# Filter spectra padded from 84 to 98 partitions with zeros

## The chip, the cores and the metric

One core of a Trainium2 chip runs the kernel. The metric is the device time in microseconds (us) of one execution. The engines are PE (TensorE), DVE (VectorE), ACT (ScalarE), POOL (GpSimd) and the queue of SP, which here only issues DMAs.

## What is computed

The reference, cut to what matters (B = 2, S = 12480, D = 128):

```python
h_filt = (np.maximum(pos_emb @ w1, 0.0) @ w2) * np.exp(-0.01 * pos)[:, None]
u = x * v
Uf = np.fft.rfft(u, n=2 * S, axis=1)
Hf = np.fft.rfft(h_filt, n=2 * S, axis=0)
y = np.fft.irfft(Uf * Hf[None], n=2 * S, axis=1)[:, :S, :]
a = (x * y).reshape(B * S, D)
h = a @ moe_w_in
out = (np.maximum(h, 0) + moe_alpha * np.minimum(h, 0)) @ moe_w_out
```

A long convolution of two sequences u with a filter h_filt, channel by channel, a gate, and then a two-layer network over 24,960 tokens.

## The kernel before, in words

The convolution is done with Fourier transforms written as matrix products. Time is split as t = 128 p + i; p lies on partitions, i along the free axis. A sequence u needs NT = 98 values of p. The filter falls by exp(-1.28) from one p to the next and is kept for HT = 84 values of p, so its operands have 84 partitions where those of u have 98. Each number is held as a high and a low half of 16 bits, so that each product is three matmuls.

The 128 channels are done in two groups (g = 0, 1) of 64. For each group there are three stages:

- **Stage 1** (`stage1`) takes "chunks" of four channels. `u_pair` loads x and v, multiplies them (L678), sums squares (ACT L681, PE L689), finds a scale (DVE L695, L332 to L334), scales (L706), and splits into halves (ACT L712, L715). `h_chunk` does a chunk of the filter. Both end in `transform`: twelve matmuls over partitions (L750 to L752; the data are the stationary operand, the table `t1` the moving one, 180 columns), then ACT writes the high half of the result to the tile `z` (L762) and DVE the low half (L765).
- **Stage 2** (`stage2`, L836 to L841) transforms over i with tables `tw` that are loaded as it goes, and multiplies by the spectrum of the filter (DVE L864, L874, POOL L869); L887 and L891 write the product back to `z`.
- **Stage 3** (`stage3`, PE L965 to L967, ACT L977, L979, DVE L982) goes back over i and stores to `g_d` in DRAM.

A group has 32 chunks of u and 16 of the filter. For g = 0 the filter is computed first (`filter_`, PE L463 to L465); its 64 channels of group 0 are left in a part of `z` that stage 1 fills later (`hz`), and those of group 1 are stored to DRAM (`h_d`, L512, four stores from a tile `hst` that is used twice). In g = 0 the 16 filter chunks come in one run between the two halves of u. In g = 1, stage 1 runs beside stage 3 of g = 0, and its filter chunks are loaded from `h_d` (L736) and come singly between those of u. From about 600 us to the end runs the two-layer network (phase B, L1219 and L1298 to L1306).

The order of the work of stages 1 and 3 on each engine is written by a planner, `Plan`: each operation is given to it with its engine, an assumed duration, what it reads and what it writes; it simulates the engines and emits the operations in the order of their simulated starts. Each engine runs its own list in order. `Plan.op` has an argument `rows` (128 unless given): for a PE operation the simulated clock is 2.4 or 1.2 GHz by the work that the simulated PE did shortly before, weighted by `rows / 128`. `pace` in `phase_a` gives each kind of work its place.

Of the kernel before, what the change touches and what calls it, by code (L numbers as in the profile page):

```python
# [24 lines left out]
NI = 128  # L25
# [262 lines left out]
def body(ctx, tc, A, out, stop=None, dbg=None):  # L288
# [27 lines left out]
    early = {}  # L316
    ring = const.tile([128, 25 - FIRST, 512], F32, name="ring")

    h_d = dram.tile([CG // CC, HT, 2, CC * NI], F16, name="h_d")
    w_d = dram.tile([NFT // 4, 128, 4, 4, 128], F16, name="w_d")  # L320
    wo_d = dram.tile([NFT // 4 - 1, 128, 512], F32, name="wo_d")
    g_d = dram.tile([64 // IDX, NF, B * D // W3, IDX * 4 * W3], F32, name="g_d")
# [17 lines left out]
    def filter_(P, pool, z, zw, mm, mb):  # L340
# [12 lines left out]
        nq_ = pool.tile([128, 16], F32, bufs=1, name="nq")  # L353
        n1 = pool.tile([128, 1], F32, bufs=1, name="n1")
        nb = pool.tile([128, 128], F32, bufs=1, name="nb")
        ac.dma_start(out=w1b, in_=A["w1b"])
        ac.dma_start(out=w2b, in_=A["w2b"])
        po.tensor_tensor(out=w2q, in0=w2b[:, 0], in1=w2b[:, 1], op=ALU.add)
# [146 lines left out]
        for x in range(2):  # L505
            for q in range(4):
                final(CG + x * HC, HC, q, dst, [("hs", 0, q), ("hs", 1, q)])
                yield
            n0 = x * HC // CC
            for h in range(2):  # L510
                def store(n0=n0, h=h):
                    sy.dma_start(out=h_d[n0:n0 + HC // CC, :, h, :].rearrange("n p e -> p n e"),  # L512
                                 in_=hst[h].rearrange("p (n c) i -> p n (c i)", c=CC))
                P.op("DMA", dma_ns(HT * HC * NI * 2), store, r=[("hs", h, q) for q in range(4)], w=[("h_d", x, h)])

# [120 lines left out]
    def phase_a():  # L636
# [15 lines left out]
        def stage1(P, g, shared, U):  # L652
            def u_pair(n):

                nps = P.buf("m")
                more = not shared and n >= NCH // 2 and n // 2 % 2
                kind = ("x2", "v2", "sq1", "uhl2") if more else ("x", "v", "sq1", "uhl")
                x, v, sq = [P.buf(kind[0]) for _ in range(2)], [P.buf(kind[1]) for _ in range(2)], P.buf(kind[2])
                b, c = divmod(n * CC, CG)
                c += g * CG  # L660
                s = s_u[:, b, c:c + 2 * CC]

                def xr(j):
                    return units(U[x[j].pool][x[j].i], p=NT)

                def vr(j):
                    return units(U[v[j].pool][v[j].i], p=NT)

                def sqr():
                    return units(U[sq.pool][sq.i], p=NT).bitcast(BF16).rearrange("p (c i) -> p c i", i=NI)  # L670

                for j in range(2):
                    def load(j=j):
                        sy.dma_start(out=xr(j), in_=A["xv"][g, n + j, :, 0, :])
                        sy.dma_start(out=vr(j), in_=A["xv"][g, n + j, :, 1, :])

                    def product(e, j=j):
                        either[e].tensor_tensor(out=xr(j), in0=xr(j), in1=vr(j), op=ALU.mult)  # L678

                    def square(j=j):  # L680
                        ac.activation(sqr()[:, j * CC:j * CC + CC].rearrange("p c i -> p (c i)"), xr(j), AF.Square)  # L681

                    P.op("DMA", dma_ns(2 * NT * 2048), load, r=stored if more else [], w=[x[j], v[j]])
                    P.op({"DVE": dve_ns(512), "POOL": 1225}, 0, product, r=[v[j]], w=[x[j]])
                    P.op("ACT", act_ns(512), square, r=[x[j], sq], w=[("sq", n, j)])

                def norm():
                    for m in range(8):
                        te.matmul(mb[nps.i][:, :128], ones[:NT], sqr()[:, :, 16 * m:16 * m + 16], start=m == 0, stop=m == 7)  # L689

                def spare(j):
                    return mb[nps.i][:, 256 + 2 * CC * j:256 + 2 * CC * (j + 1)]

                def gather():
                    ve.tensor_reduce(out=spare(0), in_=mb[nps.i][:, :128].rearrange("p (c e) -> p c e", e=16), op=ALU.add, axis=AX.X)  # L695

                def scale():
                    scales(spare(1), spare(0), s)

                P.op("PE", 450, norm, r=[sq, ("sq", n, 0), ("sq", n, 1)], w=[nps], rows=98)  # L700
                P.op("DVE", 220, gather, r=[nps], w=[("s", g, n)])
                P.op("DVE", 450, scale, r=[nps], w=[("s", g, n)])
                for j in range(2):
                    def scaled(e, j=j):
                        u = xr(j).rearrange("p (c i) -> p c i", c=CC)
                        either[e].tensor_tensor(out=u, in0=u, op=ALU.mult,  # L706
                                                in1=s[:NT, j * CC:(j + 1) * CC].unsqueeze(2).to_broadcast([NT, CC, NI]))

                    h = P.buf(kind[3])

                    def high(j=j, h=h):
                        ac.activation(halves(h)[:, 0], xr(j), AF.Copy)  # L712

                    def low(e, j=j, h=h):
                        either[e].tensor_tensor(out=halves(h)[:, 1], in0=xr(j), in1=halves(h)[:, 0], op=ALU.subtract)  # L715

                    P.op({"DVE": 600, "POOL": 1001}, 0, scaled, r=[("s", g, n)], w=[x[j]])
                    P.op("ACT", act_ns(512), high, r=[x[j]], w=[h])
                    P.op({"DVE": 600, "POOL": 1113}, 0, low, r=[x[j]], w=[h])
                    transform(n + j, [h], split(h))  # L720
# [7 lines left out]
            def h_chunk(n):  # L728
                if not shared:
                    c0 = n * CC  # L730
                    hz = z[:HT, NU // ZC:].rearrange("p b h a f c -> p b (h a f) c")
                    transform(n, [("hz", h, q) for h in range(2) for q in range(8)],
                              lambda c, part: hz[:, (c0 - NU) // ZC, part * NI:(part + 1) * NI, c0 % ZC + c])
                    return
                h = P.buf("uhl")
                P.op("DMA", dma_ns(HT * 2048), lambda: sy.dma_start(out=halves(h, HT), in_=h_d[n - NCH]), w=[h])  # L736
                transform(n, [h], split(h, HT))

            def transform(n, keys, data):
                pb = P.buf("mm")  # L740
                col = n * CC
                zb, cs = z[:, col // ZC], slice(col % ZC, col % ZC + CC)
                late = [("rs", x) for x in range(8)] if not shared and CG <= col < NU else []

                def product():
                    p = mm[pb.i].rearrange("p (c j) -> p c j", c=CC)
                    rows = HT if n >= NCH else NT
                    for c in range(CC):
                        o = p[:, c, :2 * NF]
                        te.matmul(o, data(c, 0), t1[:rows, 0], start=True, stop=False)  # L750
                        te.matmul(o, data(c, 0), t1[:rows, 1], start=False, stop=False)  # L751
                        te.matmul(o, data(c, 1), t1[:rows, 0], start=False, stop=True)  # L752

                def pv():
                    return mm[pb.i].rearrange("p (c j) -> p c j", c=CC)[:, :, :2 * NF].rearrange("p c (a f) -> p a f c", a=2)

                P.op("PE", 12 * 84, product, r=keys, w=[pb] + late, rows=98)

                cuts = (0, 2 * FB, NF) if n == NCH - 1 or shared and n == NC // CC - 1 else (0, NF)
                for x, y in zip(cuts, cuts[1:]):  # L760
                    def high(x=x, y=y):
                        ac.activation(zb[:, 0, :, x:y, cs], pv()[:, :, x:y], AF.Copy)  # L762

                    def low(x=x, y=y):
                        ve.tensor_tensor(out=zb[:, 1, :, x:y, cs], in0=pv()[:, :, x:y], in1=zb[:, 0, :, x:y, cs], op=ALU.subtract)  # L765

                    P.op("ACT", act_ns(8 * (y - x), True), high, r=[pb], w=[("z", n, x)])
                    P.op("DVE", dve_ns(8 * (y - x)), low, r=[pb], w=[("z", n, x)])
# [175 lines left out]
        def stage3(P, g, places, sines_at, y, tap=None):  # L944
            for q in range(NU // W3):
# [6 lines left out]
                for h in range(W3 // 4):  # L952
# [32 lines left out]

                    for i0, i1 in ((1, 2), (2, 64)) if tap and q == NU // W3 - 1 else ((1, 64),):
                        P.op("ACT", 2 * act_ns(4 * (i1 - i0), True) + 70 * (i0 == 1), lambda i=(i0, i1), f=sines: f(*i),
                             r=[pb, gb, *(y[1] if q == ZC // W3 - 1 else ())], w=[(sb_, i0), ("g", r, 2, i0)])
                        for k, op in enumerate((ALU.add, ALU.subtract)):
                            P.op("DVE", dve_ns(8 * (i1 - i0)), lambda k=k, op=op, i=(i0, i1), f=both: f(k, op, *i),  # L990
                                 r=[pb, sb_, (sb_, i0), gb], w=[("g", r, k, i0)])
# [415 lines left out]
```

## Time and profile before

| | us |
|---|---|
| median of three runs | 1719.01 |
| lowest and highest | 1716.59 to 1724.47 |
| profiled execution, its own time | 1721.53 |
| its span, first to last instruction | 1719.7 |

The span holds stage 1 of g = 0 from the start to about 162 us, stage 2 to about 285, stages 1 and 3 together to about 420, stage 2 of g = 1 to about 535, the last stage 3 to about 600, and phase B. In rows of the trace "84*128 84x180" is a matmul whose stationary operand has 84 partitions and 128 columns and whose moving one has 84 partitions and 180 columns. PEclk is the granted clock of TensorE as a share of 2.4 GHz: 1.00 and 0.50 are its two levels, and what lies between is a mean over a stretch that has both.

### The profile page before, as it was taken

The page shows a single profiled execution, that of the slowest core. Times are in us where ns is not written, and L with a number is a line of the kernel's source. Part 1 is how long each engine was busy: PE and PEld are TensorE (multiplying, and loading weights), DVE is VectorE, ACT ScalarE, POOL GpSimd, SP SyncE. Part 2 cuts the span into 40 slices and gives each one's busy share as a digit, 9 for nine tenths or more (in the row PEclk, how much of TensorE's full clock was granted, in tenths as well). Part 3 has the DMA queues.
Part 4 walks back from the last instruction along what each step waited for, and adds up shares of the span by engine and source line. Part 5 has one row for each costly group of instructions (what it writes and reads, how often), then busy time and mean ns, then how long its engine had stood idle before and what let it go on. Part 6 is the DMA issues. An engine that isn't in the chain of part 4 may idle for free.

```text
span 1719.7 us, 34460 instructions
## 1 busy us (share of the span) xinstructions
PE 1597.5 (93%) x13452; PEld 1128.3 (66%) x13452; DVE 1406.8 (82%) x1946; ACT 1342.8 (78%) x2227; POOL 972.6 (57%) x689
## 2 busy tenths in 40 slices
PE   6888888889888899999999999999999999999998
PEld 3887878888778756655565556555655565556654
DVE  5867998976988778888888888888888887888786
ACT  5766776776785488888888888888888888888886
POOL 5565887885895055445544554555444554555443
PEclk9867999997999999999999999999999999999999
DMA  7342334775443941120220212202202022022100
GB/s 202 109 127 93 130 123 148 219 216 165 154 150 99 245 110 52 40 54 20 72 54 20 54 37 56 54 20 61 63 22 54 20 72 54 20 54 57 36 10 20
DMA packets 95571, 144.63 MB, mean 84 GB/s; under 512 B 7187, under 2 KB 63861, under 8 KB 93967
## 3 DMA queue, kind: packets, MB, share of 16 engines
q1 hardware_dynamic: 94287, 141.72, 28.3%
q8 instruction: 105, 1.72, 0.4%
q10 hardware_dynamic: 1120, 0.70, 0.1%
q14 instruction: 59, 0.48, 0.1%
HBM read 100.39 MB, written 42.01 MB: 83 GB/s over the span
## 4 chain that ended last, share of the span: by engine, by line
PE 60%; DVE 16%; ACT 8%; issue 7%; DMA 6%; POOL 2%; SPq 0%; POOLq 0%; ACTq 0%; DVEq 0%
PE hp L1219 25%; PE o L1219 22%; DVE ring L864 4%; DVE ring L1299 4%; ACT ring L1298 3%; DVE ring L874 3%; DMA first<-in_xv 2%; ACT g_hi L1305 2%; PE mm L752 1%; DMA g_d<-ring 1%; PE mm L750 1%; PE mm L751 1%; PE yp L278 1%; PE yp L280 1%; PE yp L279 1%
## 5 line engine op out<-in xcount | busy, mean ns | idle before, releaser
L1219 PEld LDWEIGHTS <-w 128*128 128x128 f16 x6144 | 590.2, 97 | 444.2 <-issue 35.3
L1306 POOL TENSOR_TENSOR g_lo<-ring,g_hi 128x780 f16<-128x780 f32 x256 | 442.6, 1729 | 546.7 <-ACT g_hi L1305 546.5
L1299 DVE SCALAR_TENSOR_TENSOR ring<-ring,keep,hp 128x780 f32<-128x780 f32 x512 | 524.1, 1024 | 188.8 <-ACT ring L1298 182.2
L1298 ACT ACTIVATE ring<-hp 128x780 f32<-128x780 f32 x512 | 419.1, 819 | 169.1 <-PE hp L1219 168.3
L1219 PE MATMUL hp<-ah,w 128*128 128x390 f16 x2048 | 506.2, 328 | 15.2 <-DVE ring L1299 14.1
L1219 PE MATMUL o<-g_hi,w 128*128 128x390 f16 x2048 | 504.4, 328 | 0.7 <-ACT ot L1320 0.7
L1305 ACT ACTIVATE g_hi<-ring 128x780 f16<-128x780 f32 x512 | 434.0, 848 | 2.7 <-DVE ring L1299 0.8
L1306 DVE TENSOR_TENSOR g_lo<-ring,g_hi 128x780 f16<-128x780 f32 x256 | 330.2, 1290 | 0.0
L1219 PE MATMUL hp<-alo,w 128*128 128x390 f16 x1024 | 253.3, 328 | 0.8 <-DVE alo L1211 0.8
L1219 PE MATMUL o<-g_lo,w 128*128 128x390 f16 x1024 | 252.6, 328 | 0.6 <-POOL g_lo L1306 0.6
L1181 POOL TENSOR_TENSOR gl<-gt,gh 90x1024 f16<-90x1024 f32 x62 | 132.7, 2141 | 0.0
L864 DVE TENSOR_TENSOR ring<-mm,ring 128x512 f32<-128x512 f32 (+2 forms) x188 | 115.9, 656 | 15.4 <-ACT ring L852 14.7
L891 POOL TENSOR_TENSOR z<-ring,z 128x512 f16<-128x512 f32 x88 | 110.5, 1256 | 7.2 <-ACT z L887 7.2
L765 DVE TENSOR_TENSOR z<-mm,z 128x720 f16<-128x720 f32 (+1 forms) x99 | 85.7, 878 | 33.1 <-ACT z L762 32.8
L965 PE MATMUL mm<-t,z 128*128 128x128 f16 x512 | 103.5, 234 | 8.2 <-DVE ring L982 3.9
L750 PE MATMUL mm<-t,ring 98*128 98x180 f16 (+1 forms) x320 | 88.3, 278 | 24.5 <-DVE z L765 7.7
L869 POOL TENSOR_TENSOR ring<-ring 128x256 f32<-128x256 f32 (+1 forms) x90 | 80.6, 896 | 48.4 <-DVE ring L864 40.1
L762 ACT ACTIVATE z<-mm 128x720 f16<-128x720 f32 (+1 forms) x99 | 74.2, 756 | 39.4 <-PE mm L752 39.1
L966 PE MATMUL mm<-t,z 128*128 128x128 f16 x512 | 102.9, 233 | 0.0
L967 PE MATMUL mm<-t,z 128*128 128x128 f16 x512 | 102.8, 233 | 0.0
L982 DVE TENSOR_TENSOR ring<-mm,ring 90x504 f32<-90x504 f32 (+2 forms) x132 | 80.7, 656 | 22.7 <-ACT ring L979 21.9
L715 POOL TENSOR_TENSOR ring<-ring 98x512 f16<-98x512 f32 x63 | 79.1, 1272 | 27.8 <-ACT ring L712 24.6
(186 smaller groups left out, 2999.2 us busy)
## 6 DMA issues: line engine op xcount, KB each, us to landing
g_d<-ring SPq DMA_DIRECT2D x32, 720.0 KB
gt<-g_d SPq DMA_DIRECT2D x16, 1440.0 KB
ring<-in_tw SPq DMA_DIRECT2D x34, 512.0 KB
ring<-in_xv SPq DMA_DIRECT2D x72, 196.0 KB
xt<-in_xt SPq DMA_DIRECT2D x31, 390.0 KB
out_t<-ot SPq DMA_DIRECT2D x31, 390.0 KB
first<-in_xv SPq DMA_DIRECT2D x56, 196.0 KB
first<-in_tw SPq DMA_DIRECT2D x12, 512.0 KB
```

The source lines that it names most:

```text
L750: te.matmul(o, data(c, 0), t1[:rows, 0], start=True, stop=False)
L864: ve.tensor_tensor(out=t[:, :, m], in0=p[:, :, m], in1=hs[:, a:a + 1, m].to_broadcast([128, 2, (b1 - b0) * 2 * ZC]), op=ALU.mult)
L891: e.tensor_tensor(out=zl, in0=v, in1=zh, op=ALU.subtract)
L965: te.matmul(o, hi, t3[:, 0], start=True, stop=False)
L966: te.matmul(o, hi, t3[:, 1], start=False, stop=False)
L967: te.matmul(o, lo, t3[:, 0], start=False, stop=True)
L1181: po.tensor_tensor(out=dl, in0=src, in1=dh, op=ALU.subtract)
L1219: te.matmul(o[:, b, :TOK], w, d[:, b], start=start and n == 0, stop=stop and n == 2)
L1298: ac.activation(neg, h, AF.Relu, scale=-1.0)
L1299: ve.scalar_tensor_tensor(out=acts[n], in0=neg, scalar=keep[:, f:f + 1], in1=h, op0=ALU.mult, op1=ALU.add)
L1305: ac.activation(gh, a, AF.Copy)
L1306: (ve, po)[n % 2].tensor_tensor(out=gl, in0=a, in1=gh, op=ALU.subtract)
```

## The change

The filter's operands are laid out with 98 partitions, the last 14 zero, and all transforms read 98. `hz` is cleared once from partition 64 up at the start (one memset on DVE, one on POOL), before `filter_` writes its 84. `h_d` has 98 partitions, and one more DMA writes zeros to 14 of them. The planner's arguments change too: `rows=98` is dropped for the two PE operations of stage 1, the transform is put down with 78 in place of 84 ns for a matmul, and in `stage3` the wait of ACT for the end of stage 2 (`y[1]`) stands at the second block of eight channels in place of the fourth.

```diff
-    h_d = dram.tile([CG // CC, HT, 2, CC * NI], F16, name="h_d")
+    h_d = dram.tile([CG // CC, NT, 2, CC * NI], F16, name="h_d")
...
+        zero = pool.tile([NT - HT, 2 * CC * NI], F16, bufs=1, name="zero")
+        po.memset(zero, 0.0)
+        for b, e in ((0, ve), (1, po)):
+            e.memset(zw.bitcast(F32)[64:, (NU // ZC + b) * 2 * NF * ZC:][:, :NI * ZC], 0.0)
...
+            if x == 0:
+                P.op("DMA", dma_ns((NT - HT) * CG * NI * 4), lambda: sy.dma_start(
+                    out=h_d[:, HT:].rearrange("n p h e -> p n (h e)"),
+                    in_=zero.unsqueeze(1).to_broadcast([NT - HT, CG // CC, 2 * CC * NI])), r=[("hs", 0, 0)], w=[("h_d", 2, 0)])
...
-                    sy.dma_start(out=h_d[n0:n0 + HC // CC, :, h, :].rearrange("n p e -> p n e"),
+                    sy.dma_start(out=h_d[n0:n0 + HC // CC, :HT, h, :].rearrange("n p e -> p n e"),
...
-                P.op("PE", 450, norm, r=[sq, ("sq", n, 0), ("sq", n, 1)], w=[nps], rows=98)
+                P.op("PE", 450, norm, r=[sq, ("sq", n, 0), ("sq", n, 1)], w=[nps])
...
-                    hz = z[:HT, NU // ZC:].rearrange("p b h a f c -> p b (h a f) c")
+                    hz = z[:NT, NU // ZC:].rearrange("p b h a f c -> p b (h a f) c")
...
-                P.op("DMA", dma_ns(HT * 2048), lambda: sy.dma_start(out=halves(h, HT), in_=h_d[n - NCH]), w=[h])
-                transform(n, [h], split(h, HT))
+                P.op("DMA", dma_ns(NT * 2048), lambda: sy.dma_start(out=halves(h), in_=h_d[n - NCH]), w=[h])
+                transform(n, [h], split(h))
...
-                        te.matmul(o, data(c, 0), t1[:rows, 0], start=True, stop=False)
+                        te.matmul(o, data(c, 0), t1[:, 0], start=True, stop=False)
...
-                P.op("PE", 12 * 84, product, r=keys, w=[pb] + late, rows=98)
+                P.op("PE", 12 * 78, product, r=keys, w=[pb] + late)
...
-                             r=[pb, gb, *(y[1] if q == ZC // W3 - 1 else ())], w=[(sb_, i0), ("g", r, 2, i0)])
+                             r=[pb, gb, *(y[1] if q == 1 else ())], w=[(sb_, i0), ("g", r, 2, i0)])
```

## Rows read from the trace of the kernel before

**Rows 1.** The page: busy time by engine; granted clock in 40 slices of 43 us.

```profile
PE 1597.5 (93%) x13452; PEld 1128.3 (66%) x13452; DVE 1406.8 (82%) x1946; ACT 1342.8 (78%) x2227; POOL 972.6 (57%) x689
...
PEclk9867999997999999999999999999999999999999
```

**Rows 2.** Stretches: from:to, length, busy us (x instructions) of engines, clock, DMA.

```profile
110.00:120.00 10.00, 10.00 (x72) 10.00 (x70) 4.83 (x6) 5.93 (x9) 3.05 (x3) 0.50 0.11 34
...
140.00:150.00 10.00, 7.69 (x67) 6.87 (x65) 9.90 (x15) 7.60 (x13) 10.00 (x9) 0.75 0.69 237
...
410.00:420.00 10.00, 9.61 (x63) 9.17 (x62) 4.85 (x7) 5.62 (x10) 2.57 (x3) 0.50 0.48 165
...
106.80:133.20 26.40, 26.40 (x187) 26.39 (x186) 14.77 (x28) 15.60 (x24) 14.73 (x14) 0.50 0.10 32
...
309.50:400.40 90.90, 79.73 (x1082) 76.43 (x1080) 77.27 (x141) 66.64 (x156) 75.52 (x64) 0.97 0.77 224
```

**Rows 3.** Groups by shape, 104 to 133.2 us: busy us, mean ns, idle before.

```profile
L752 PE MATMUL mm<-t,z 84*128 84x180 f16 x52 | 18.5, 356 | 0.0
...
L765 DVE TENSOR_TENSOR z<-mm,z 128x720 f16<-128x720 f32 x16 | 14.4, 904 | 10.8 <-ACT z L762 10.7
L762 ACT ACTIVATE z<-mm 128x720 f16<-128x720 f32 x15 | 11.7, 778 | 12.3 <-PE mm L752 12.3
```

**Rows 4.** Timeline of PE: start us, us; a run of 72 matmuls.

```profile
107.86 0.36 PE L750 MATMUL mm<-t,z 84*128 84x180 f16 x1
...
118.50 0.36 PE L752 MATMUL mm<-t,z 84*128 84x180 f16 x1
```

**Rows 5.** Timeline of PE after the filter chunks: two stretches of 98-partition matmuls.

```profile
130.22 0.36 PE L750 MATMUL mm<-t,ring 98*128 98x180 f16 x1
...
134.85 0.24 PE L751 MATMUL mm<-t,ring 98*128 98x180 f16 x1
...
136.63 0.24 PE L750 MATMUL mm<-t,ring 98*128 98x180 f16 x1
...
137.49 0.24 PE L752 MATMUL mm<-t,ring 98*128 98x180 f16 x1
```

**Rows 6.** Timeline of PE, then of DVE, at the gap ahead of the filter chunks.

```profile
101.65 0.31 PE L750 MATMUL mm<-t,ring 98*128 98x180 f16 x1 [4.70 <-DVE z L765]
...
100.08 0.69 DVE L678 TENSOR_TENSOR ring<-ring 98x512 f32<-98x512 f32 x1 [4.41 <-DMA ring<-in_xv]
```

**Rows 7.** Groups by shape, 404 to 419.6 us: busy us, mean ns, idle before.

```profile
L752 PE MATMUL mm<-t,ring 98*128 98x180 f16 x21 | 7.5, 357 | 0.0
...
L765 DVE TENSOR_TENSOR z<-mm,z 128x720 f16<-128x720 f32 x7 | 6.3, 906 | 5.5 <-ACT z L762 5.5
...
L750 PE MATMUL mm<-t,ring 84*128 84x180 f16 x12 | 4.3, 358 | 0.0
```

**Rows 8.** Timeline of PE, SP's queue and DVE at the end of stage 1.

```profile
400.44 0.25 PE L750 MATMUL mm<-t,ring 84*128 84x180 f16 x1 [2.69 <-DMA ring<-h_d]
...
401.92 12.31 SPq L736 DMA_DIRECT2D ring<-h_d  x3
...
422.44 0.43 DVE L532 TENSOR_SCALAR ring<-ring 128x512 int32<-128x512 int32 x1 [1.27 <-DMA ring<-in_wo]
```

**Rows 9.** Timelines of DVE and POOL at the start of the span.

```profile
1.02 0.20 DVE L386 MEMSET z<- 128x176 uint32 x1
5.10 0.51 DVE L405 SCALAR_TENSOR_TENSOR z<-mm,ring 128x336 f32<-128x336 f32 x1 [3.87 <-PE mm L402]
...
12.20 1.26 POOL L678 TENSOR_TENSOR ring<-ring,first 98x512 f32<-98x512 f32 x1 [6.90 <-DMA first<-in_xv]
```

**Rows 10.** The chain in order of time, 60 to 180 us; DMA issues there.

```profile
75.82 5.50 DMA h_d<-ring
...
h_d<-ring SPq DMA_DIRECT2D x4, 672.0 KB
```

**Rows 11.** Timelines of DVE and ACT where stage 3 of g = 0 begins.

```profile
291.52 0.78 DVE L891 TENSOR_TENSOR z<-ring,z 128x384 f16<-128x384 f32 x1
...
292.06 0.66 ACT L977 ACTIVATE ring<-mm 90x252 f32<-90x252 f32 x2 [0.33 <-PE mm L967]
```

More of the change, by code (lines that the diff above doesn't have):

```diff
@@ L746, in product @@
                     p = mm[pb.i].rearrange("p (c j) -> p c j", c=CC)
-                    rows = HT if n >= NCH else NT
                     for c in range(CC):
                         o = p[:, c, :2 * NF]
-                        te.matmul(o, data(c, 0), t1[:rows, 0], start=True, stop=False)
-                        te.matmul(o, data(c, 0), t1[:rows, 1], start=False, stop=False)
-                        te.matmul(o, data(c, 1), t1[:rows, 0], start=False, stop=True)
+                        te.matmul(o, data(c, 0), t1[:, 0], start=True, stop=False)
+                        te.matmul(o, data(c, 0), t1[:, 1], start=False, stop=False)
+                        te.matmul(o, data(c, 1), t1[:, 0], start=False, stop=True)
                 def pv():
                     return mm[pb.i].rearrange("p (c j) -> p c j", c=CC)[:, :, :2 * NF].rearrange("p c (a f) -> p a f c", a=2)
-                P.op("PE", 12 * 84, product, r=keys, w=[pb] + late, rows=98)
+                P.op("PE", 12 * 78, product, r=keys, w=[pb] + late)
                 cuts = (0, 2 * FB, NF) if n == NCH - 1 or shared and n == NC // CC - 1 else (0, NF)
```

## The prediction

> **What bounds the kernel now.** I read the page first. PE is busy 93% of the span, but its clock is not high throughout: in the 40 slices it stands at 9 nearly everywhere and falls to 6 and 7 in the third, fourth and tenth [rows 1]. Those slices lie in stage 1 of g = 0 and at the end of stage 1 of g = 1, where the filter's transforms are. So next the busy times by stretch, to see what binds there: from 106.8 to 133.2 us PE is busy for all 26.40 us at 0.50, which is 1.2 GHz, while DVE, ACT and POOL each work for only some 15 us; 410 to 420 looks alike [rows 2]. Then the groups of that first stretch, to see who waits for whom: before the DVE evictions L765 lie 10.8 us of idle time, ended by ACT L762, and before those 12.3 us, ended by PE L752 [rows 3]. That is a loop with PE at its head: PE is the bound, at half its clock. From 140 to 150 us, in the second half of u, it is the other way round, DVE 9.90 and POOL 10.00 of 10 us [rows 2]; a faster PE buys nothing there.
>
> The timeline shows what the clock did. It fell behind a PE gap of 4.70 us, which a late load of x and v opened [rows 6]. Then filter chunks with 84 partitions ran back to back: 72 matmuls from 107.86 to 118.50, one each 10.64/71 = 0.150 us, and the clock did not rise [rows 2, 4]. At 130.22 chunks with 98 partitions took over, equally dense, and 4.6 us later, at 134.85, a matmul lasted 0.24 in place of 0.36 us: the clock had risen [rows 5]. From then twelve matmuls come one each 0.86/11 = 0.078 us [rows 5]. Of what PE did before, the number of partitions is the one plain difference between the two streams.
>
> **The change part by part.**
>
> **The 98 partitions in g = 0.** The count and columns of the matmuls stay. A chunk takes 12 x 0.150 = 1.80 us at the low clock and 12 x 0.078 = 0.94 at the high one [rows 4, 5]. I assume that the gap before 101.65 stays, so the clock still falls, but that the stream which follows now has 98 partitions throughout and lifts it after 4.6 us, at 106.3, in place of 134.85. Of those 28.5 us PE alone would give back 28.5 x (1 - 0.078/0.150) = 13.7. It will not all come: DVE has 14.77 us of work in 26.4, thus about 16 in 28.5, so it becomes the bound and at most 12.5 come back [rows 2]. The upper end is 12.5. The lower: the chunks of u behind the filter must be loaded, scaled and split meanwhile on the same engines, and if they are ready no earlier than now, the gain ends in a wait ahead of them; only what shortens the loads' waits is left, which I bound by a quarter, 3. These products wait in their queues behind the evictions that wait for PE, so most of the chain moves along, and I take 9.0, nearer to the DVE row than to nothing.
>
> **The 98 partitions in g = 1.** From 309.5 to 400.4 the clock is 0.97 [rows 2], so there is next to nothing to get. At 400.44 a gap of 2.69 us, for a filter chunk from DRAM, ends that [rows 8], and up to 419.6 chunks of 98 and 84 partitions alternate at 0.36 us a matmul [rows 7]. With 98 throughout, a rise 4.6 us after 400.44 would come at 405; I put it at 406.5, since the clock has first to fall and a short wait may start the count anew. Then 13 us are left, PE saving at most 13 x 0.48 = 6.2. DVE idles 5.5 us of that stretch for want of ACT and so of PE [rows 7], so it could follow. But the tables of stage 2 are queued on SP behind three filter loads that wait 12.31 us for their buffers, and DVE then stands 1.27 us for a load behind these tables [rows 8]: transfers of fixed length take part of it back. Between 2 and 6.2 I take 4.5. Stage 2 would also start at the high clock: its first 24 matmuls, of 192 columns, would take 24 x 0.072 x 192/180 = 1.8 us less, an estimate from rows 4 and 5. The same transfers cover that, and I count nothing; without them the forecast would be 1.8 lower.
>
> **The memsets.** Each clears 4096 words on 64 partitions. DVE's 176 words took 0.20 us [rows 9], so at that rate 4.7 us, from 1.2 to 5.9; the first relu stands at 5.10, after 3.87 us of idle time. It is at most 0.8 us late, and POOL's first product still waits for its load until 12.20; 0. POOL has no wide memset in the trace: at the rate of its 512-word product (1.26 us) this one and the zero tile are 5120 words, 12.6 us; at DVE's rate 5.8. POOL is nearly idle until 12.20, where it waits for a load [rows 9]. So 0, or 2 us if it is the slow rate and all of that gets through; I take 0.
>
> **The DMAs.** The zero store moves 14/84 of the four stores' 4 x 672 KB, 448 KB. The first store stands on the chain for 5.50 us [rows 10], since `hst` can be rewritten only when it has left. The zero store is placed close ahead of it on SP's queue. Fully in its way it costs 448/672 x 5.50 = 3.7; if it falls into the idle DMA time before, 0. I take 1.0. The filter loads grow from 168 to 196 KB, sixteen times 28 KB; at 224 GB/s in that stretch [rows 2] 2.0 us if all of it were on the path, and I take 0.3, since only the load at 400.44 held PE up.
>
> **The wait in stage 3.** The third of ACT's groups L977 starts at 292.06, when the last DVE write of stage 2, 291.52 + 0.78 = 292.30, is nearly done [rows 11]. Now it must be planned behind it: 0.2 to 1 us, once; 0.2, within the rounding.
>
> **The planner's figures.** With 128 rows and 78 ns it believes PE faster, and emits some operations in another order. No row prices that; I take 0 and widen the range by 5 us to both sides.
>
> **The sum.** 9.0 + 4.5 - 1.0 - 0.3 = 12.2 us less. The profiled execution took 1721.5, which gives 1709.3; it lay 2.5 above the median of the runs, so against 1719.0 the forecast is 1707.
>
> **The rivals.**
>
> *The lift comes, but others are late instead* (DVE, POOL and the loads of u). Lower ends, 3 and 2, less 1.3: 1715. For it: POOL and DVE are full right behind, at 140 to 150 us [rows 2]. Against: half their time ahead of it is idle.
>
> *The clock does not rise at 98 partitions of filter.* The rows show that 98 partitions of u lift it; those of the filter hold exp(-1.28 p), nearly zero in most partitions, and the 14 new ones are exactly zero. If it is values that count, the stream stays at 0.50, and the costs remain: 1719 + 1.3 = 1720. Against: nothing decisive; in rows 5 partitions and values changed together. The Trainium skill, TensorE: Matmul & The Clock Gate, Part 1, speaks for this rival: there sustained activity alone releases the clock, and rows of the operand are not named. By that, the dense 84-partition stream should already have risen, which this trace contradicts with 0.50 for 26.4 us [rows 2], so I give the page little weight.
>
> *Slower: the new order breaks the dense stretch of g = 1.* From 309.5 to 400.4 PE holds 0.97 with 79.7 us of busy time in 90.9 [rows 2], amid stage 3, loads and u. If the planner, counting on a faster PE, puts evictions ahead of the products that feed PE, gaps open and the clock falls there as at 101.65. All of it at 0.50 would need 79.7 x 0.97/0.50 = 155 us, 64 more than there are. It decides once a third of the stretch is lost: 21 - 12 = 9 slower, 1728. Against: PE's places there are set by `pace`, which is unchanged, and stage 3, with 128 partitions, is between.
>
> **How the numbers follow.** The forecast 0.60, its own range 1699 to 1713; others late 0.18; no lift 0.13; slower 0.09. About 0.5% (8.6 us) is what a measurement can tell from no change. Faster by more than that: nearly all of the forecast, 0.54, and 0.04 of the second case: 0.58. Slower: the last rival and a little of the third, 0.10. The rest is 0.32. The range is 1695 to 1720: the forecast with the planner's 5 us, the second case, and half the third.
>
> **What would show it.** Right: the clock between 107 and 130 us and 407 and 419 near 1.00, L750 at 0.24 us there with 98 partitions, DVE's idle time before L765 gone, the start of stage 2 about 8 us earlier than 162 and again about 12 earlier than 420. Wrong: 0.50 in the filter chunks (third case); the clock high but new PE idle time at 120 to 145 ended by POOL L715 or loads (second); the clock under 0.9 from 300 to 400 (last).

## The result, and the profile after

The changed kernel takes 1700.85 us (median of four runs, 1695.17 to 1703.11) where the kernel before takes 1719.23 beside it: a ratio of 0.9884, 95% interval 0.985 to 0.9918, 18 us less. The forecast was 1707, 12 us less, with a range of 1695 to 1720. The profiled execution (1695.17, span 1693.4) is the fastest of its four, and that of before lies 2.3 above its median, so stretches of the two traces differ by 26 us together where the medians differ by 18. The experiments below, which are more executions of the same stretches, say which differences hold.

The page after: busy time by engine, and the granted clock in 40 slices of 42 us [compare rows 1].

```profile
PE 1574.1 (93%) x13452; PEld 1103.2 (65%) x13452; DVE 1410.4 (83%) x1948; ACT 1340.5 (79%) x2227; POOL 976.7 (58%) x690
...
PEclk9899998999999899999999999999999999999999
```

The 6 and 7 are gone. PE has 23 us less busy time for the same number of matmuls, and its weight loads 25 us less; DVE, ACT and POOL change by 2 to 4 us.

Stretches after: from:to, length, busy time of PE, PEld, DVE, ACT and POOL, clock, DMA [compare rows 2].

```profile
110.00:120.00 10.00, 9.63 (x128) 9.48 (x127) 9.59 (x23) 9.61 (x16) 9.96 (x10) 1.00 0.26 83
130.00:140.00 10.00, 5.16 (x39) 4.76 (x40) 9.57 (x19) 5.05 (x10) 8.41 (x7) 0.69 0.30 109
...
102.60:115.80 13.20, 12.53 (x167) 12.46 (x166) 12.79 (x26) 12.75 (x22) 9.88 (x10) 0.99 0.23 73
```

In the filter chunks the clock is up, and all four engines are full: 110 to 120 us, which now takes in the first chunks of u behind them, holds 128 matmuls in place of 72. PE is no longer the one bound; from 102.6 to 115.8 us DVE and ACT are level with it. The second row is the sign that was given for the rival in which others are late: from 130 to 140 us PE is busy for half the time, and the clock falls again.

Timeline of PE at the gap ahead of the filter chunks (start us, us), and the groups by shape from 102.6 to 115.8 us (busy us, mean ns, idle before) [compare rows 3 to 6].

```profile
99.28 0.24 PE L757 MATMUL mm<-t,z 98*128 98x180 f16 x1 [3.48 <-DVE z L772]
...
102.14 0.36 PE L757 MATMUL mm<-t,z 98*128 98x180 f16 x1
...
103.18 0.24 PE L759 MATMUL mm<-t,z 98*128 98x180 f16 x1
```

```profile
L759 PE MATMUL mm<-t,z 98*128 98x180 f16 x45 | 10.8, 243 | 0.0
...
L772 DVE TENSOR_TENSOR z<-mm,z 128x720 f16<-128x720 f32 x12 | 10.4, 898 | 0.4 <-ACT z L769 0.2
L769 ACT ACTIVATE z<-mm 128x720 f16<-128x720 f32 x12 | 9.1, 790 | 0.5 <-PE mm L759 0.5
```

The gap is still there, and the clock falls behind it; but now it is up again at 103.18, and the idle time ahead of the evictions, 10.8 and 12.3 us in [rows 3], is down to 0.4 and 0.5.

The added work, in timelines of DVE, POOL and SP's queue:

```profile
1.92 3.47 DVE L359 MEMSET z<- 64x4096 f32 x1 [0.92 <-issue]
5.60 0.45 DVE L409 SCALAR_TENSOR_TENSOR z<-mm,ring 128x336 f32<-128x336 f32 x1
7.29 0.51 DVE L409 SCALAR_TENSOR_TENSOR z<-mm,ring 128x336 f32<-128x336 f32 x1 [1.25 <-PE mm L406]
```

```profile
1.72 3.51 POOL L359 MEMSET z<- 64x4096 f32 x1
...
12.13 1.26 POOL L686 TENSOR_TENSOR ring<-ring,first 98x512 f32<-98x512 f32 x1 [5.88 <-DMA first<-in_xv]
```

```profile
57.22 0.40 SPq L515 DMA_DIRECT2D h_d<-zero  x1
66.35 0.32 SPq L682 DMA_DIRECT2D ring<-in_xv  x1
...
70.58 3.46 SPq L520 DMA_DIRECT2D h_d<-ring  x2
```

Each memset takes 3.5 us. The first relu is 0.5 us late [rows 9], the next waits for PE again, and POOL still waits for its load. The zero store goes out at 57.22, and the next transfer on this queue comes 9 us later, so nothing behind it waits. The two loads queued just ahead of it share the time with it; what that costs them is not shown by itself.

Where the stages begin, in the two traces:

| first matmul of | before | after | gained up to here |
|---|---|---|---|
| filter chunks after the gap (for before, one chunk of u ahead of them) | 101.65 | 99.28 | 2.4 |
| chunks of u behind them | 130.22 | 115.78 | 14.4 |
| stage 2, g = 0 | 162.12 | 144.09 | 18.0 |
| stage 3, g = 0 | 286.39 | 267.99 | 18.4 |
| stage 2, g = 1 | 419.61 | 393.40 | 26.2 |
| phase B | 600.37 | 575.00 | 25.4 |

### The profile page after: what moved, and what is told of

Same layout as the page of the kernel before. It is cut to its first block, busy times and chain, and to the rows that moved or that the text cites. A ratio compares the mean times of both kernels' runs of the same rounds, so it can differ in the third digit from the quotient of the medians.

```text
span 1693.4 us, 34477 instructions
## 1 busy us (share of the span) xinstructions
PE 1574.1 (93%) x13452; PEld 1103.2 (65%) x13452; DVE 1410.4 (83%) x1948; ACT 1340.5 (79%) x2227; POOL 976.7 (58%) x690
## 4 chain that ended last, share of the span: by engine, by line
PE 59%; DVE 16%; ACT 9%; issue 8%; DMA 4%; POOL 4%; SPq 0%; POOLq 0%; ACTq 0%; DVEq 0%
PE hp L1226 25%; PE o L1226 22%; DVE ring L871 4%; DVE ring L1306 4%; ACT ring L1305 3%; DVE ring L881 3%; POOL ring L723 2%; ACT g_hi L1312 2%; DMA first<-in_xv 1%; PE yp L278 1%; PE yp L279 1%; PE yp L280 1%; PE mm L972 1%; DVE g_lo L1313 1%; PE mm L974 1%
## 5 line engine op out<-in xcount | busy, mean ns | idle before, releaser
L1226 PE MATMUL hp<-ah,w 128*128 128x390 f16 x2048 | 506.4, 328 | 14.4 <-DVE ring L1306 13.3
L757 PE MATMUL mm<-t,ring 98*128 98x180 f16 x320 | 81.3, 257 | 18.5 <-DVE z L772 5.8
L772 DVE TENSOR_TENSOR z<-mm,z 128x720 f16<-128x720 f32 (+1 forms) x99 | 84.9, 876 | 12.3 <-ACT z L769 11.8
L769 ACT ACTIVATE z<-mm 128x720 f16<-128x720 f32 (+1 forms) x99 | 73.6, 756 | 26.2 <-PE mm L759 25.7
L894 ACT ACTIVATE z<-ring 128x512 f16<-128x512 f32 (+2 forms) x94 | 57.2, 609 | 45.3 <-DVE ring L881 33.5
```

The costliest lines, as they stand in the source:

```text
L1226: te.matmul(o[:, b, :TOK], w, d[:, b], start=start and n == 0, stop=stop and n == 2)
```

## The experiments

The theory: a dense stream of matmuls with 84 partitions does not bring the clock back once it has fallen, one with 98 does, whatever the values in them; that is the gain. The rivals: the planner's new order makes the gain; the gain is in g = 1 as much as in g = 0; the values, not the partitions, count.

**The padding without the planner's figures, and these without the padding.** `pad_only` is the changed kernel with

```diff
-                P.op("PE", 450, norm, r=[sq, ("sq", n, 0), ("sq", n, 1)], w=[nps])
+                P.op("PE", 450, norm, r=[sq, ("sq", n, 0), ("sq", n, 1)], w=[nps], rows=98)
...
-                P.op("PE", 12 * 78, product, r=keys, w=[pb] + late)
+                P.op("PE", 12 * 84, product, r=keys, w=[pb] + late, rows=98)
...
-                             r=[pb, gb, *(y[1] if q == 1 else ())], w=[(sb_, i0), ("g", r, 2, i0)])
+                             r=[pb, gb, *(y[1] if q == ZC // W3 - 1 else ())], w=[(sb_, i0), ("g", r, 2, i0)])
```

> Padding as in the changed kernel, the planner's three figures as before (98 rows, 84 ns, the wait of ACT at the fourth block). Theory A, the 98 partitions alone make the gain: 1701 us, within 3 of the changed kernel, the filter chunks of g = 0 near clock 1.00. Rival B, the new order of operations makes a third of it: about 1707, as forecast for the padding alone.

`plan_only` is the kernel before with the same three lines changed the other way.

> 84 partitions as before, the planner's three figures as in the changed kernel. Theory A: 1719, within 4 of the kernel before, filter chunks of g = 0 at clock 0.50 for some 25 us. Rival B: 1711 to 1714, since part of the gain comes with the order.

Measured: `pad_only` 1700.42 us, ratio to before 0.9895 (0.9872 to 0.9917). `plan_only` 1714.7, ratio 0.9969 (0.9955 to 0.9983), close to the upper end of what rival B said. Stretch 110 to 120 us of `pad_only`:

```profile
110.00:120.00 10.00, 8.73 (x115) 8.46 (x113) 9.25 (x18) 9.29 (x17) 8.99 (x9) 1.00 0.24 83
```

The padding with the three figures as before gives the whole gain. The new order alone is worth 4.5 us, which theory A did not allow for; but it adds nothing that can be measured to the padding: the two do not sum. One thing is left open: `pad_only` does not keep the order of before throughout, since the planner is told of the zero store and of larger filter loads too. PE's matmuls come in the order of before up to 293 us, thus all through g = 0; from there to 397 us, 256 of the 13,452 places differ. What that is worth was not measured.

**The padding in one group only.** `pad_g0` reads the filter chunks of g = 1 with 84 partitions and has no zero store; `pad_g1` reads those of g = 0 with 84 and has no memsets of `hz`. Cut to the core:

```diff
+            def transform(n, keys, data, rows=NT):
...
-                        te.matmul(o, data(c, 0), t1[:, 0], start=True, stop=False)
+                        te.matmul(o, data(c, 0), t1[:rows, 0], start=True, stop=False)
...
-                transform(n, [h], split(h))
+                transform(n, [h], split(h, HT), HT)
```

(the last pair for `pad_g0`; in `pad_g1` the call on `hz` gets `HT`.)

> The changed kernel, but the filter chunks of g = 1 are read from DRAM with 84 partitions, without the zero store. If the gain of g = 1 is from the clock there, its end of stage 1 stays at 0.50 as before: 1701 + 6 = 1707. If it is only order and shorter waits in g = 1: 1701.

> The changed kernel, but the filter chunks of g = 0 are read with 84 partitions, without the memsets. If the clock in g = 0 is worth what the traces of before and after show between 101 and 130 us, 12 us come back: 1713. If g = 0 gained by order instead, 1704 or less.

Measured: `pad_g0` 1699.96, ratio 0.9891 (0.9871 to 0.9911); `pad_g1` 1708.03, ratio 0.9942 (0.992 to 0.9964). Stretch 110 to 120 us of `plan_only`, then `pad_g0`, then `pad_g1`:

```profile
110.00:120.00 10.00, 10.00 (x72) 10.00 (x71) 5.98 (x13) 5.80 (x11) 4.25 (x4) 0.50 0.09 26
```

```profile
110.00:120.00 10.00, 9.63 (x126) 9.46 (x125) 9.60 (x22) 9.60 (x16) 9.80 (x10) 1.00 0.25 83
```

```profile
110.00:120.00 10.00, 10.00 (x73) 10.00 (x71) 5.71 (x13) 6.11 (x10) 4.26 (x4) 0.50 0.06 16
```

With one order of operations, the 98 partitions switch the stretch from 0.50 to 1.00 and back: PE's matmuls come in one and the same order in `pad_g0`, `pad_g1` and the changed kernel, and `plan_only` differs from it only in 32 places at 314 to 320 us.

The padding of g = 0 alone reaches the time of the changed kernel, 14.7 us less than `plan_only`; the 6 us that `pad_g0` was to lose for g = 1 did not show. But g = 1 is not worth nothing. `pad_g1` lies between the two values given for it, 1713 and 1704: with the padding of g = 1 alone the kernel is 6.7 us faster than `plan_only` (medians of six and twelve executions; 5.4 by their means), and that of g = 0 on top is then worth 7 to 9 us in place of 12. So the two paddings do not sum either: 14.7 and 6.7 us alone, 14 to 16 together. Why they do not is open. The trace of `pad_g1` is little help: it is of the slowest of its six executions (1714.34), and takes some 4 us more than that of `plan_only` behind stage 3, where the two kernels do the same.

What the padding does in g = 1 is seen at the end of its stage 1, from the last matmul of stage 3 to the first of stage 2, in `plan_only` and in the changed kernel:

```profile
390.50:414.40 23.90, 19.11 (x167) 18.03 (x166) 14.33 (x25) 13.62 (x26) 14.94 (x14) 0.71 0.49 150
```

```profile
372.90:393.40 20.50, 16.68 (x167) 15.10 (x166) 14.19 (x25) 13.62 (x26) 15.02 (x14) 0.83 0.50 152
```

In the new order the clock comes back in that stretch with 84 partitions too: in `plan_only` it falls at 396.25, is up from 406.49 to 409.91 and again from 413.32, where in the kernel before it fell at 401.07 and stayed at 0.50 to the end of the stretch [rows 2]. What brings it back there is not shown; 98-partition products of u stand between those of the filter in both. Padding shortens the stretch only from 23.9 to 20.5. The other traces of the new order agree: from the end of the last matmul of stage 3 it is 23.2 and 23.5 us with 84 partitions, and 19.6 to 22.2 with 98.

The stages in all profiled executions, in us (run of the filter chunks: from the gap to the first chunk of u behind them; in the old order this holds one chunk of u more; the order of `pad_only` is the old one in g = 0 alone):

| kernel | order | filter, g = 0 / g = 1 | run of filter chunks | u behind it | stage 1 of g = 0 ends | stages 1 and 3 of g = 1 |
|---|---|---|---|---|---|---|
| before | old | 84 / 84 | 28.6 | 31.9 | 162.1 | 133.2 |
| pad_only | old | 98 / 98 | 19.1 | 31.3 | 148.5 | 122.8 |
| plan_only | new | 84 / 84 | 26.8 | 31.9 | 160.5 | 129.4 |
| pad_g1 | new | 84 / 98 | 26.5 | 32.2 | 161.1 | 125.6 |
| pad_g0 | new | 98 / 84 | 16.6 | 31.0 | 146.8 | 128.0 |
| changed | new | 98 / 98 | 16.5 | 28.3 | 144.1 | 125.4 |
| changed_again | new | 98 / 98 | 16.8 | 28.2 | 145.5 | 129.2 |
| zeros | new | 98 / 98 | 17.6 | 28.1 | 147.1 | 125.8 |
| r128 | new | 128 / 98 | 16.2 | 28.3 | 146.1 | 125.9 |
| g0_128 | new | 128 / 98 | 16.3 | 28.5 | 147.6 | 126.9 |
| half98 | new | 98, then 84 / 98 | 17.4 | 30.1 | 148.3 | 127.8 |

**The changed kernel again**, measured beside the next three.

> The changed kernel as it is, beside the others of this call and with more runs. 1700 to 1702. If the padding of g = 1 is worth nothing on top of that of g = 0, it is no faster than 1700, where the kernel padded in g = 0 alone stands; if it is worth the 3 us that the two profiled executions differ by, 1697.

1698.74 us, ratio 0.9887 (0.9871 to 0.9903), against 0.9891 (0.9871 to 0.9911) for `pad_g0`: the times cannot tell whether the padding of g = 1 does anything on top of that of g = 0. The table says little more: the stages of g = 1 take 126.7 us as a mean over seven executions of the new order with 98 partitions there (125.4 to 129.2) and 128.7 over two with 84 (128.0 and 129.4). That would be some 2 us, as the end of stage 1 alone says too, but the two sets overlap.

**Zeros in every partition.** `zeros` is the changed kernel with the filter's spectra written as exact zeros by the same instructions:

```diff
-                    ac.activation(d, p, AF.Copy)
+                    ac.activation(d, p, AF.Copy, scale=0.0)
...
-                    ve.tensor_tensor(out=d, in0=p, in1=h, op=ALU.subtract)
+                    ve.tensor_tensor(out=d, in0=p, in1=h, op=ALU.mult)
```

> The changed kernel with every filter operand written as exact zeros by the same instructions (the convolution is then zero; all else runs as before). Theory, partitions count and not values: the clock still rises within 7 us of the gap at 99 us and stays at 1.00 through the filter chunks, which last as long as in the changed kernel, some 16.5 us. Rival, values count: 0.50 through the chunks, some 27 us.

One run, 1697.14 us. Timeline of PE in the filter chunks, then the stretch behind the rise:

```profile
101.49 0.24 PE L757 MATMUL mm<-t,z 98*128 98x180 f16 x1 [3.48 <-DVE z L772]
...
103.05 0.31 PE L757 MATMUL mm<-t,z 98*128 98x180 f16 x1 [0.34 <-DVE z L772]
103.16 0.36 PE L758 MATMUL mm<-t,z 98*128 98x180 f16 x1
...
109.22 0.24 PE L757 MATMUL mm<-t,z 98*128 98x180 f16 x1
...
110.00:120.00 10.00, 10.00 (x138) 10.00 (x136) 9.27 (x22) 10.00 (x17) 8.24 (x8) 1.00 0.25 84
```

A stationary operand that is zero everywhere brings the clock back as well, here 6.1 us after the dense stream began and 7.7 after the end of the gap, a little more than the 7 that were given. The filter chunks last 17.6 us, and 1.00 holds through the rest of them. So in this one execution it is the partitions that an instruction names, not what is in them. This was the rival "the clock does not rise at 98 partitions of filter", and it falls.

**More partitions.** `r128` reads the filter of g = 0 with all 128, `g0_128` the chunks of u of g = 0 too; `t1` gets 30 rows of zeros.

```diff
-                    hz = z[:NT, NU // ZC:].rearrange("p b h a f c -> p b (h a f) c")
+                    hz = z[:, NU // ZC:].rearrange("p b h a f c -> p b (h a f) c")
...
+        for u, k in ((11, 4), (23, 2)):
+            po.memset(units(u, k)[64:], 0.0)
...
-                    transform(n + j, [h], split(h))
+                    transform(n + j, [h], split(h) if shared else split(h, 128), NT if shared else 128)
```

(the last two pairs for `g0_128` only.)

> The changed kernel, but the filter chunks of g = 0 are read with all 128 partitions (the table's rows past 98 are zero, the memsets cover them already). If more partitions lift the clock sooner, the 3 us at 0.50 behind the gap at 99 us shrink by 1 to 2: 1699. Else 1700.5.

> As r128, and the chunks of u of g = 0 are read with 128 partitions too (rows past 98 cleared at the start). If the clock then keeps up at 120 to 145 us, where 98 partitions still fell to 0.69, stage 2 of g = 0 starts 2 to 4 us earlier: 1697. If the wait there is for POOL and loads alone: 1700.

1696.39 us, ratio 0.9874 (0.9853 to 0.9894), and 1699.2, ratio 0.9885 (0.9867 to 0.9903): neither differs from the changed kernel by more than the intervals, though 1696.39 is below both values given for it. More partitions do not lift the clock sooner: it was at 0.50 for 3.4 us behind the gap in both, and for 3.4 and 6.8 us in the two executions of the changed kernel. The run of filter chunks is 16.2 and 16.3 us, and what is left at 120 to 145 us stays: in `g0_128` as in the changed kernel PE waits there 2.31 us for DVE's scales (L334), 1.2 for ACT's halves and 2.01 for POOL's, with 128 partitions as with 98. None of these kernels is measurably faster than the changed one.

**To lift it, or to hold it?** `half98` reads the first nine filter chunks of g = 0 with 98 partitions and the last seven with 84:

```diff
+                    rows = NT if n < NCH + 9 else HT
-                    hz = z[:NT, NU // ZC:].rearrange("p b h a f c -> p b (h a f) c")
+                    hz = z[:rows, NU // ZC:].rearrange("p b h a f c -> p b (h a f) c")
```

> The changed kernel, but of the 16 filter chunks of g = 0 only the first nine (three ahead of the gap, six behind it) are read with 98 partitions, the other seven with 84. If 98 partitions are needed only to lift the clock and 84 hold it once it is up, the seven run at 0.078 us a matmul and the time is that of the changed kernel, 1699. If 84 partitions also let it fall, they run at 0.150 and some 5 us come back: 1704.

1698.48 us, ratio 0.9876 (0.9852 to 0.99), the time of the changed kernel. First and last of the 84 matmuls with 84 partitions, and the stretch that holds most of them:

```profile
109.91 0.24 PE L758 MATMUL mm<-t,z 84*128 84x180 f16 x1
...
117.65 0.24 PE L760 MATMUL mm<-t,z 84*128 84x180 f16 x1
...
111.30:117.90 6.60, 6.57 (x88) 6.45 (x84) 6.24 (x14) 6.60 (x12) 6.20 (x7) 1.00 0.27 84
```

All run at 0.24 us. Once the clock is up, 84 partitions hold it over these 8 us; they only fail to bring it back. The 84 matmuls come in runs of at most 36, with eight short 98-partition products (L697) between; the same mixture held the clock here and did not lift it in 26 us of `plan_only`. A longer run of 84 partitions alone was not tried at the high clock. This fits the kernel before, which ran filter chunks between those of u at 0.97 from 309 to 400 us [rows 2] and stayed at 0.50 behind a gap.

## Why the prediction was right, and where its sizes were off

- *PE is the bound in the filter chunks, at half its clock, and 98 partitions lift it.* Right, and shown with the order of operations held: 0.50 in `plan_only` and `pad_g1`, 1.00 in `pad_g0`, at the same place.
- *g = 0: 9.0 of at most 12.5 us.* The run of filter chunks became shorter by 9.5 us in the old order (28.6 to 19.1) and by 10.1 in the new (26.7 to 16.6, means of `plan_only` and `pad_g1`, and of `pad_g0`, changed and changed_again). The mechanism was right, and this part of the step was sized right. What was missed lies behind it: the chunks of u take 28.3 us where they took 31.9, in the five executions of seven of the new order in which the clock survives a PE wait of about 2 us at 122 to 128 us, and 30.1 and 31.0 in the two in which it does not. The 1 to 2 us that are left even in those two fit the first chunks of u, which ran at 0.50 up to 134.85 before and lay within the forecast's 28.5 us; the other 2 to 3 contradict "a faster PE buys nothing there". The end of stage 1 of g = 0 moved from 160.8 (mean of `plan_only` and `pad_g1`) to 146.5 (mean of the seven with 98 or more): 14 us in place of 9, as the 14.7 of `pad_g0` against `plan_only` say too, above the upper end of 12.5. About 1.4 of the 14 are there before the gap ends. The reading of the slices was wrong in one place: the fourth (129 to 172 us) lies mostly behind the filter chunks, in the second half of u.
- *g = 1: 4.5.* It depends on g = 0, which the forecast did not allow for: 6.7 us alone, a little above the 6.2 that were given, and nothing that the times can tell on top of g = 0, where the table would allow some 2. For the old order one execution each of before and `pad_only` says 10.4, with PE's order changed as well; stage 2 behind it gave 4.2 back (118.8 to 123.0 us). This much of the idea that transfers of fixed length take back a part may hold, but its cause was not traced.
- *The zero store, 1.0, and larger loads, 0.3.* The store was not close ahead of the first store but 13 us ahead of it (57.22 and 70.58), with nothing queued right behind; the end of 0 was given and not taken. `pad_g0`, which has neither, is not measurably faster than the kernels that have both, though it lacks what the padding of g = 1 may bring as well.
- *The memsets, 0.* Right; at 3.5 us each they are quicker than both bounds.
- *The planner's figures, 0, 5 us to both sides.* Alone they give 4.5 us, on top of the padding nothing. Why the two do not sum is not settled. The table shows where, by one execution for each kernel of the old order: there g = 1 gains more than in the new one, in the new one the chunks of u do.
- *Others are late instead.* DVE and ACT did become level with PE, 12.79 and 12.75 of 13.2 us, but at 1.3 us a chunk, where `plan_only` and `pad_g1` take 2.1, both with what lies between the chunks. The second sign given for this case, new PE idle time behind the filter, is there too (2.02, 2.31, 1.22 and 2.01 us from 122 to 136 us, ended by DVE, ACT and POOL); it cost less than the chunks of u gained. *Slower by a broken stretch in g = 1*: no such stretch; the slices of g = 1 stand at 9 and 8. The start of stage 2, given as about 8 and 12 us earlier in the two groups, is 18.0 and 26.2 earlier in the two traces.

So 12.2 was too small by 6. The two paddings together are worth 14 to 16 us on top of the new order, where 13.5 were given; the costs of 1.3 do not show; and the order adds 4.5 alone, where 0 was given with 5 to both sides. These do not add up to a ledger, since the parts overlap: that the sum came as close as it did is in part luck. The 2.4 us that the trace of before is later at the gap are of unknown cause. The gap ends at 101.7 to 102.5 us in the three traces with 84 partitions in g = 0 and at 98.1 to 102.7 in the eight others; most of the difference is already there at the first filter chunk, before any padded matmul, and the changed kernel alone scatters by 1.1 us in two executions.

The forecast doubted the Trainium skill, TensorE: Matmul & The Clock Gate, Part 1, where sustained activity alone releases the clock. The runs uphold the doubt: 13 filter chunks of 84 partitions, dense for 26 us with short 98-partition products between them, did not release it in `plan_only` and `pad_g1`, and the same instructions with 98 did, with zeros in them too.

## What to carry to other kernels

Where a busy PE stands at 1.2 GHz, look at how many partitions its matmuls name, not only for gaps: here a stream of 84 could hold the clock but not win it back after a wait, one of 98 could, and zeros were enough to widen it. Where between 84 and 98 the difference sets in was not measured. Rows of zeros cost no PE time here (0.24 us a matmul with 84 as with 98), so the price is the clearing and the larger transfers, which here fitted into idle time. In `half98` the 72 wide matmuls of the six chunks behind the gap did the same as padding all of that stream. And what two such repairs are worth has to be measured together: each alone was worth more than it added to the other.

## What the hardware showed that was not expected

All-zero stationary operands bring the clock back too. Counted from the end of the gap it rose after 7.7 us with them and after 3.4 to 6.3 us in the seven other kernels with 98 partitions or more behind it; it was at 0.50 for 6.8 us, as in four of the seven (3.4 us in three), so nothing here shows zeros to be slower. A wait of 2.0 us ahead of 98-partition chunks let the clock fall in `pad_g0` and `half98`, and not in five others with the same order of operations:

```profile
124.12 0.31 PE L751 MATMUL mm<-t,ring 98*128 98x180 f16 x1 [2.04 <-DVE z L766]
124.23 0.36 PE L752 MATMUL mm<-t,ring 98*128 98x180 f16 x1
```

```profile
124.13 0.24 PE L757 MATMUL mm<-t,ring 98*128 98x180 f16 x1 [2.02 <-DVE z L772]
124.21 0.24 PE L758 MATMUL mm<-t,ring 98*128 98x180 f16 x1
```

The first is `pad_g0`, the second the changed kernel; the 3 us between them are in the column "u behind it" of the table. A single profile of such a stretch is worth no more than that.
